# ScalarE's issue order in the attention stage: the next square and the weight casts queue behind the copies of scores, keys and x

## The chip, the cores and the metric

One core of a Trainium2 chip runs the whole kernel as one program. The metric is the device time in microseconds (us). Before the change the median of three runs is 611.57 us (609.62 to 613.83).

## The reference, cut to what matters

Three blocks follow one another, all in float32, with 4 batches, 768 tokens, 8 heads of 48 channels (d_model 384) and a hidden width of 1024:

```python
state = zeros((B, H, D, D))                         # gated linear attention
for t in range(S):
    state = alpha[:, :, t, :, None] * state + einsum('bhd,bhe->bhde', k[:, :, t], v[:, :, t])
    y[:, :, t] = einsum('bhd,bhde->bhe', q[:, :, t], state)
x = y.transpose(0, 2, 1, 3).reshape(B, S, H * D)

theta = x @ w_theta                                 # spectral block
zr, zi = x * cos(theta), x * sin(theta)
u = x + einsum('ts,bsd->btd', w_tok_r, zr) + einsum('ts,bsd->btd', w_tok_i, zi)
x = u + maximum(u @ w_ch, 0)

h = maximum(x @ w_in, 0)                            # gated block: 3-tap convolution over tokens
out = (h * sigmoid(conv3(h, conv_w))) @ w_out
```

## The kernel before, in words

**Attention by chunks.** The 24 chunks are 4 batches times 6 chunks of 128 tokens; chunk numbers below run from 0 to 23 over all batches. `a_prep` (L198) works on one chunk's keys and queries: VectorE runs two scans over the gates (L210, L215) into the tile `fbt`, of which there is one buffer, and multiplies queries and keys by them (L218). ScalarE then squares `fbt` in place and sums it (L219); the sum serves only a test of the number range at the end of the kernel, but the next chunk's first scan writes the same buffer and so comes after the square. `a_score` (L222) forms the scores on TensorE; ScalarE copies them out of PSUM into two tiles `pt` (L232; two buffers in all, so one chunk's), GpSimd masks them (L233); TensorE transposes the keys and ScalarE copies them to `kt` (L241, one buffer). `a_y` (L244) forms the chunk's output `y` from `pt`, the values and the state `S`; ScalarE copies it to `x` (L259). TensorE forms `kv`, VectorE adds it to the state (L268, tile `tst`) and GpSimd scales it into the next `S` (L273). `a_xt` (L280) transposes `x`, and ScalarE copies the transpose into `u` (L290). `a_theta` (L292) splits `u` in two float32r halves (`zh`, L71 and L72), multiplies by w_theta (`th`), and makes the two products with cosine and sine, again split (`zh`, `zl`). `m_mix` (L322) multiplies those by the token weights `wtok` into `yps`.

**Weights.** `load_split` (L105) fetches a block of 8-byte words into a `stage` tile, of which there are two, decodes it on VectorE (`decode`, L101 to L103), casts the upper half on ScalarE and forms the rest on VectorE (`split`, L70: L71 and L72). The 12 blocks of the token weights (`load_tok`, 6 for each half of the tokens) and the two of w_theta pass through the two stage tiles with the tag "st", in batch 0 and 1 of the attention. A stage tile is free for the next fetch once L72 has read it.

**Order.** In the code, `a_att(b, c)` starts the loads of chunk ci + 2, then prepares and scores chunk ci + 1, then finishes chunk ci. For batch 0 each `a_att(0, c)` is followed by `load_tok(0, c)`; for batch 1 by `load_tok(1, c)`. A planner, which simulates the program with its own cost model, turns this into one fixed queue for each engine: of the instructions that are ready it takes the one that stands first in the code. Each engine works its queue in that order, and an instruction at the head that waits holds up what stands behind it. Batches 1 to 3 of the attention are interleaved with the token mixing of the batch before; what follows 330 us holds no attention.

Of the kernel before, what the change touches and what calls it, by code (L numbers as in the profile page):

```python
# [14 lines left out]
AF = mybir.ActivationFunctionType  # L15
# [3 lines left out]
P = 128  # L19
# [24 lines left out]
def tile_gated_linear_attention__then__spectral_moe__then__conv_gate(  # L44
# [14 lines left out]
    nc = tc.nc  # L59
    NCH = B * NC  # L60

    def mm(o, lhsT, rhs, start, stop):
        nc.tensor.matmul(o, lhsT, rhs, start=start, stop=stop, skip_group_check=True)  # L63
# [4 lines left out]
        mm(o, a[1], b[0], False, stop)  # L68

    def split(hi, lo, src, lo_eng):  # L70
        nc.scalar.copy(hi, src)  # L71
        lo_eng.tensor_tensor(lo, src, hi.bitcast(F32), ALU.subtract)  # L72

    top_p = ctx.enter_context(tc.tile_pool(name="top", bufs=1))
    dram_p = ctx.enter_context(tc.tile_pool(name="xd", bufs=1, space=bass.MemoryType.DRAM))
    wmin = top_p.tile([P, NTOP], F32, name="wmin")
    bacc = top_p.tile([P, NCH], F32, name="bacc")
# [3 lines left out]
    def run(slow):  # L81
        with ExitStack() as top:
            body(top, slow)

    def body(top, slow):
# [19 lines left out]
        def load_split(pool, tag, src, shape, out_hi, out_lo, scale=None):  # L105
            n = math.prod(shape)
            st = pool.tile([P, 9 * 256], F32, tag=tag, name="stage", bufs=STB)
            d = st[:, : 2 * n].bitcast(U32)
            if len(shape) == 2:
                d = d.rearrange("p (a n) -> p a n", a=shape[0])  # L110
            nc.sync.dma_start(out=d, in_=src)
            full = st[:, 1536 : 1536 + n]
            decode(full, st, n)
            if scale is not None:
                nc.scalar.activation(full, full, AF.Copy, scale=scale)
            if len(shape) == 2:
                full = full.rearrange("p (a n) -> p a n", a=shape[0])
            split(out_hi, out_lo, full, nc.vector)

        ub, xs, zs = {}, {}, {}  # L120

# [2 lines left out]
        with ExitStack() as ph1:  # L124
# [13 lines left out]
            def load_tok(h, c):  # L138
                hs = slice(h * HALF, (h + 1) * HALF)
                load_split(  # L140
                    u_p,
                    "st",
                    w_tok[:, c * P : (c + 1) * P, hs].rearrange("i p t -> p i t").bitcast(U32),
                    [2, HALF],
                    wtok[h][0][:, :, c, :],
                    wtok[h][1][:, :, c, :],
                )
# [50 lines left out]
            def a_prep(ci):  # L198
                at, qt, vt = raw.pop(ci)
                qr = qt[:, 0:CW]  # L200
                kr = qt[:, CW : 2 * CW]
                ff = at[:, 0:CW]
                ash = at[:, 1 : CW + 1]
                ast = at[:, CW + 1 : CW + 5]
                fbt = sc_p.tile([P, 2, CW], F32, tag="fbt", name="fbt")
                fo, bf = fbt[:, 0], fbt[:, 1]
                bt = bf.rearrange("p (a t) -> p a t", a=4)
                of = onehot.rearrange("p a t -> p (a t)")
                ftot = att.tile([P, 4], F32, tag="ftot", name="ftot")
                nc.vector.tensor_tensor_scan(  # L210
                    bf[:, CW - 1 :: -1], ash[:, CW - 1 :: -1], of[:, CW - 1 :: -1], 0.0, ALU.mult, ALU.add
                )
                nc.vector.tensor_scalar(starts[:, :, 0], bt[:, :, 0], LEAST, None, ALU.max)
                nc.vector.reciprocal(starts[:, :, 0], starts[:, :, 0])
                nc.vector.tensor_tensor_scan(fo, ff, starts.rearrange("p a t -> p (a t)"), 0.0, ALU.mult, ALU.add)  # L215
                nc.vector.tensor_tensor(ftot, ast, bt[:, :, 0], ALU.mult)
                fl = fbt.rearrange("p b t -> p (b t)")
                nc.vector.tensor_tensor(qt, qt, fl, ALU.mult)  # L218
                nc.scalar.activation(fl, fl, AF.Square, accum_out=bacc[:, ci : ci + 1])  # L219
                prep[ci] = (qr.rearrange("p (a t) -> p a t", a=4), kr.rearrange("p (a t) -> p a t", a=4), ftot, vt)  # L220

            def a_score(ci):  # L222
                qh, kh, ftot, vt = prep[ci]
                scs = [ps_a.tile([P, NP, P], F32, tag="a", name="sc") for _ in range(2)]
                for p in range(NP):
                    for j in range(2):
                        r = slice(64 * j, 64 * j + D)
                        mm(scs[j][:, p, :], kh[r, p, :], qh[r, p, :], True, True)
                pts = []
                for j in range(2):  # L230
                    pt = att.tile([P, NP, P], F32, tag="pt", name="pt")
                    nc.scalar.copy(pt, scs[j])  # L232
                    nc.gpsimd.affine_select(pt, pt, [[0, NP], [1, P]], ALU.is_ge, 0.0, base=0, channel_multiplier=-1)  # L233
                    pts.append(pt)
                kt = None
                if ci % NC < NC - 1:
                    kps = ps_a.tile([P, 4, P], F32, tag="a", name="kps")
                    for p in range(NP):
                        nc.tensor.transpose(kps[:, p, :], kh[:, p, :], ident)  # L239
                    kt = att.tile([P, 4, P], F32, tag="kt", name="kt", bufs=1)  # L240
                    nc.scalar.copy(kt, kps)  # L241
                scored[ci] = (pts, kt)

            def a_y(ci):  # L244
                qh, kh, ftot, vt = prep.pop(ci)
                pts, kt = scored.pop(ci)
                c = ci % NC
                Sp, Sn = Sst[ci % 2], Sst[(ci + 1) % 2]
                y = ps_a.tile([P, DM], F32, tag="a", name="y")
                first = True  # L250
                for p in range(NP):
                    for j in range(2):
                        h = 2 * p + j
                        mm(y[:, h * D : (h + 1) * D], pts[j][:, p, :], vt[:, h * D : (h + 1) * D], first, c == 0)
                        first = False
                    if c > 0:
                        mm(y[:, p * 96 : p * 96 + 96], qh[:, p, :], Sp[:, p, :], False, True)
                x = x_p.tile([P, DM], F32, tag="x", name="x")
                nc.scalar.copy(x, y)  # L259
                xs[ci] = x  # L260
                if c < NC - 1:
                    kv = ps_a.tile([P, NP, 2 * D], F32, tag="a", name="kv")
                    for p in range(NP):
                        mm(kv[:112, p, :], kt[:, p, :112], vt[:, p * 96 : p * 96 + 96], p == 0, True)
                    nft = prep[ci + 1][2]
                    if c > 0:
                        tt = att.tile([P, NP, 2 * D], F32, tag="tst", name="tst", bufs=1)
                        nc.vector.tensor_tensor(tt[:112], Sp[:112], kv[:112], ALU.add)  # L268
                    else:
                        tt = kv  # L270
                    for j in range(2):
                        r = slice(64 * j, 64 * j + D)
                        (nc.gpsimd if c > 0 else nc.vector).tensor_tensor(  # L273
                            Sn[r, :, j * D : (j + 1) * D],
                            tt[r, :, j * D : (j + 1) * D],
                            nft[r].unsqueeze(2).to_broadcast([D, NP, D]),
                            ALU.mult,
                        )

            def a_xt(ci):  # L280
                b, c = divmod(ci, NC)
                if c == 0:
                    late = b >= B - STB
                    ub[b] = u_p.tile(
                        [P, KD, S], F32, tag="st" if late else "u", name="u", bufs=STB if late else B - STB
                    )
                xps = ps_a.tile([P, KD, P], F32, tag="a", name="xps")
                for kk in range(KD):
                    nc.tensor.transpose(xps[:, kk, :], xs[ci][:, kk * P : (kk + 1) * P], ident)
                nc.scalar.copy(ub[b][:, :, c * P : (c + 1) * P], xps)  # L290

            def a_theta(ci):  # L292
                b, c = divmod(ci, NC)
# [80 lines left out]
            for b in range(B - 1):  # L374
                for c in range(NC):
                    m_mix(b, 0, c)
                    a_att(b + 1, c)
                    if b == 0:
                        load_tok(1, c)
                for c in range(NC):  # L380
                    m_mix(b, 1, c)
                    a_theta((b + 1) * NC + c)
            att_ctx.close()
            ps_n = top.enter_context(tc.tile_pool(name="ps_n", bufs=5, space=PSUM))
            w_p = top.enter_context(tc.tile_pool(name="w2", bufs=1, side="right"))
# [271 lines left out]
```

## Time and profile before

| | |
|---|---|
| median of 3 runs | 611.57 us (609.62 to 613.83) |
| the profiled execution | 610.02 us, span of its instructions 608.3 us |
| TensorE busy, share of the span | 584.0 us, 96% |
| VectorE busy | 459.9 us, 76% |
| ScalarE busy | 333.3 us, 55% |
| GpSimd busy | 71.1 us, 12% |
| TensorE's granted clock, mean | 0.953 of full speed |

The profile is one execution. PE is TensorE's multiplications, PEld its weight loads, DVE VectorE, ACT ScalarE, POOL GpSimd, SP the queue that issues DMAs. A row of a timeline has the start in us, the length in us, the engine, the line, the operation, the tile written and the tiles read; in brackets stand the idle time of the engine before it and what ended it. PEclk is the clock granted to TensorE, where 1.00 is 2.4 GHz and 0.50 is 1.2 GHz. Matrix products of 32-bit floats are issued as two instructions each, those of float32r as one.

### The profile page before, as it was taken

The numbers are of one execution on the slowest core, as the hardware profiler recorded it, in microseconds if no ns is written. First come the engines' busy times: TensorE is split into PE (matmuls) and PEld (weight loads), VectorE is DVE, ScalarE is ACT, GpSimd is POOL, SyncE is SP. The second block draws the span as 40 slices with busy tenths as digits, with TensorE's granted clock in tenths as the row PEclk, the third lists the DMA queues.
The fourth block names the chain that finished last, engine by engine and source line by source line (L and its number), as shares of the span: only waits on it lengthen the run. The fifth ranks groups of instructions, "written<-read, shape, count | busy, mean of one in ns | idle before, by whom it ended". The sixth has DMA issues, their size and how long they took to land.

```text
span 608.3 us, 9546 instructions
## 1 busy us (share of the span) xinstructions
PE 584.0 (96%) x3703; PEld 569.2 (94%) x3703; DVE 459.9 (76%) x744; ACT 333.3 (55%) x663; POOL 71.1 (12%) x91
## 2 busy tenths in 40 slices
PE   5789999899999999999999999999999999999996
PEld 2689888799999999999999999999999999999995
DVE  7699999976764567643156888998888888888781
ACT  3436766444682446733265343666776767766571
POOL 1023621432001330112100000000000000000000
PEclk8557899899999999999999999999999999999999
DMA  8356464343102431021001333430023535445111
GB/s 297 116 176 215 151 222 127 125 138 112 62 19 77 131 119 48 15 66 61 1 0 74 110 106 105 122 138 13 27 79 117 194 118 182 148 152 194 55 41 44
DMA packets 24981, 65.33 MB, mean 107 GB/s; under 512 B 2528, under 2 KB 8672, under 8 KB 24544
## 3 DMA queue, kind: packets, MB, share of 16 engines
q1 hardware_dynamic: 24928, 64.64, 32.3%
q8 instruction: 31, 0.51, 0.3%
q14 instruction: 22, 0.18, 0.1%
HBM read 59.92 MB, written 4.72 MB: 106 GB/s over the span
## 4 chain that ended last, share of the span: by engine, by line
PE 83%; DVE 11%; DMA 2%; issue 1%; ACT 1%; POOL 1%; ACTq 0%; DVEq 0%
PE yps L63 23%; PE hps L63 17%; PE ops L63 16%; PE y L63 8%; PE cps L63 6%; PE th L63 5%; PE sc L63 3%; PE kv L63 2%; DMA stage<-in_w_tok_dram 2%; DVE fbt L215 2%; DVE fbt L210 1%; PE kps L239 1%; DVE qk_t L218 1%; DVE stage L102 1%; DVE wtok L72 1%
## 5 line engine op out<-in xcount | busy, mean ns | idle before, releaser
L63 PE MATMUL yps<-wtok,zh 128*128 128x384 f32 x576 | 151.6, 343 | 1.0 <-ACT zh L71 1.0
L63 PEld LDWEIGHTS yps<-wtok,zh 128*128 128x128 f32 x576 | 105.9, 192 | 1.7 <-ACT zh L71 1.4
L63 PE MATMUL hps<-x,win 128*128 128x386 f32 x576 | 107.1, 339 | 0.0
L63 PE MATMUL ops<-wout,g 128*128 128x384 f32 x576 | 106.9, 338 | 0.0
L63 PEld LDWEIGHTS hps<-x,win 128*128 128x128 f32 x576 | 102.2, 189 | 0.0
L63 PEld LDWEIGHTS ops<-wout,g 128*128 128x128 f32 x576 | 101.7, 187 | 0.0
L63 PE MATMUL yps<-wtok,zl 128*128 128x384 f32 x288 | 97.9, 344 | 0.0
L233 POOL TENSOR_SCALAR_AFFINE_SELECT pt<-pt 128x512 f32<-128x512 f32 x48 | 46.0, 981 | 214.9 <-ACT pt L232 214.9
L63 PE MATMUL y<-v_t,pt 128*128 128x48 f32 x384 | 59.2, 286 | 0.0
L63 PEld LDWEIGHTS y<-v_t,pt 128*128 128x128 f32 x384 | 56.3, 213 | 0.5
L63 PEld LDWEIGHTS yps<-wtok,zl 128*128 128x128 f32 x288 | 55.2, 192 | 0.0
L219 ACT ACTIVATE fbt<-fbt 128x1024 f32<-128x1024 f32 x24 | 25.4, 1059 | 52.8 <-DVE qk_t L218 52.5
L479 ACT ACTIVATE cv<-cv 128x384 f32<-128x384 f32 x64 | 33.4, 523 | 31.0 <-DVE cv L476 30.9
L72 DVE TENSOR_TENSOR g<-cv,g 128x384 fp32r<-128x384 f32 x64 | 35.4, 555 | 15.1 <-ACT g L71 14.5
L63 PE MATMUL th<-wth,zh 128*128 128x384 f32 x216 | 44.3, 348 | 0.0
L232 ACT COPY pt<-sc 128x512 f32<-128x512 f32 x48 | 25.7, 585 | 29.7 <-PE y L63 29.7
L210 DVE TENSOR_TENSOR_SCAN fbt<-a_t,onehot 128x512 f32<-128x512 f32 x24 | 29.7, 1236 | 16.3 <-ACT fbt L219 14.4
L63 PEld LDWEIGHTS sc<-qk_t 48*128 48x128 f32 x384 | 28.6, 204 | 14.0 <-issue 7.5
L63 PE MATMUL sc<-qk_t 48*128 48x128 f32 x384 | 33.8, 304 | 8.0 <-DVE qk_t L218 8.0
L473 DVE SCALAR_TENSOR_TENSOR cv<-hh,cw,cv 128x383 f32<-128x383 f32 (+1 forms) x64 | 38.3, 612 | 4.1 <-ACT cv L470 3.8
L63 PE MATMUL y<-S,qk_t 128*128 128x96 f32 x160 | 37.5, 319 | 3.9 <-POOL S L273 3.9
L480 DVE SCALAR_TENSOR_TENSOR cv<-cv,hh 128x384 f32<-128x384 f32 x64 | 35.2, 555 | 7.9 <-ACT cv L479 5.9
(84 smaller groups left out, 903.5 us busy)
## 6 DMA issues: line engine op xcount, KB each, us to landing
qk_t<-in_qka_dram SPq DMA_DIRECT2D x24, 512.0 KB, 3.7
stage<-in_w_tok_dram SPq DMA_DIRECT2D x12, 768.0 KB, 4.9
top<-in_w_tok_dram SPq DMA_DIRECT2D x12, 768.0 KB, 4.3
a_t<-in_qka_dram SPq DMA_DIRECT2D x24, 260.0 KB, 2.8
v_t<-in_v_dram SPq DMA_DIRECT2D x24, 192.0 KB, 3.3
out_dram<-ob SPq DMA_DIRECT2D x24, 192.0 KB, 1.9
stage<-in_w_in_dram SPq DMA_DIRECT2D x4, 768.0 KB, 5.1
stage<-in_w_out_dram SPq DMA_DIRECT2D x4, 768.0 KB, 4.3
```

The costliest lines, as they stand in the source:

```text
L63: nc.tensor.matmul(o, lhsT, rhs, start=start, stop=stop, skip_group_check=True)
L72: lo_eng.tensor_tensor(lo, src, hi.bitcast(F32), ALU.subtract)
L102: nc.vector.scalar_tensor_tensor(fb, hi, 0xC0000000, fb, ALU.bitwise_and, ALU.bitwise_or)
L210: nc.vector.tensor_tensor_scan(bf[:, CW - 1 :: -1], ash[:, CW - 1 :: -1], of[:, CW - 1 :: -1], 0.0, ALU.mult, ALU.add)
L215: nc.vector.tensor_tensor_scan(fo, ff, starts.rearrange("p a t -> p (a t)"), 0.0, ALU.mult, ALU.add)
L218: nc.vector.tensor_tensor(qt, qt, fl, ALU.mult)
L219: nc.scalar.activation(fl, fl, AF.Square, accum_out=bacc[:, ci : ci + 1])
L232: nc.scalar.copy(pt, scs[j])
L233: nc.gpsimd.affine_select(pt, pt, [[0, NP], [1, P]], ALU.is_ge, 0.0, base=0, channel_multiplier=-1)
L473: nc.vector.scalar_tensor_tensor(cv[:, a:HALF], hh[:, o + a - 1 : o + HALF - 1], cw[:, f, 0:1], cv[:, a:HALF], ALU.mult, ALU.add)
L479: nc.scalar.activation(cv, cv, AF.Tanh, scale=0.5)
L480: nc.vector.scalar_tensor_tensor(cv, cv, 1.0, hh[:, o : o + HALF], ALU.add, ALU.mult)
```

## The change: four copies are marked, and two kinds of instruction queue behind the marks

While the program is traced, the last copy to `pt` (L232, the second of the chunk's two), the last copy to `kt` (L241), to `x` (L259) and to `u` (L290) are remembered. Each square (L219) and each cast of a weight block with the tag "st" (L71 of `load_split`) gets an edge to those four as they stand when it is traced. The edge is of a kind that the planner honours as an order in the queue; it adds no semaphore, since all these instructions run on ScalarE. No instruction is added or removed. By the order of the code, the square of chunk n comes behind pt and kt of chunk n-1 and x and u of chunk n-2; the cast of `load_tok(0, c)` behind pt and kt of chunk c+1 and x and u of chunk c; the cast of `load_tok(1, c)` behind pt and kt of chunk c+7 and x and u of chunk c+6; the casts of w_theta behind pt and kt of chunk 1 and x and u of chunk 0.

```diff
     def split(hi, lo, src, lo_eng):
-        nc.scalar.copy(hi, src)
+        cast = nc.scalar.copy(hi, src)
         lo_eng.tensor_tensor(lo, src, hi.bitcast(F32), ALU.subtract)
+        return cast
+
+    marks = {}
+
+    def behind(ins, keys):
+        for k in keys:
+            if k in marks:
+                tc.add_manual_dep(
+                    ins.ins,
+                    marks[k].ins.name,
+                    mybir.DependencyInfo(mybir.DependencyClass.NoSync, mybir.DependencyReason.DATA),
+                    reason="issue order",
+                )
...
-            split(out_hi, out_lo, full, nc.vector)
+            cast = split(out_hi, out_lo, full, nc.vector)
+            if tag == "st" and not slow:
+                behind(cast, ("pt", "kt", "x", "u"))
...
-                nc.scalar.activation(fl, fl, AF.Square, accum_out=bacc[:, ci : ci + 1])
+                sq = nc.scalar.activation(fl, fl, AF.Square, accum_out=bacc[:, ci : ci + 1])
+                behind(sq, ("pt", "kt", "x", "u"))
...
-                    nc.scalar.copy(pt, scs[j])
+                    marks["pt"] = nc.scalar.copy(pt, scs[j])
...
-                    nc.scalar.copy(kt, kps)
+                    marks["kt"] = nc.scalar.copy(kt, kps)
...
-                nc.scalar.copy(x, y)
+                marks["x"] = nc.scalar.copy(x, y)
...
-                nc.scalar.copy(ub[b][:, :, c * P : (c + 1) * P], xps)
+                u_copy = nc.scalar.copy(ub[b][:, :, c * P : (c + 1) * P], xps)
+                if not slow:
+                    marks["u"] = u_copy
...
+            marks.clear()
             att_ctx.close()
```

## Rows read from the trace of the kernel before

**Rows 1.** Windows: busy us (instructions) of PE, PEld, DVE, ACT, POOL; PEclk, DMA, GB/s

```profile
25.00:120.00 95.00, 86.40 (x567) 81.96 (x568) 92.41 (x129) 52.60 (x98) 31.56 (x24) 0.81 0.56 176
120.00:370.00 250.00, 250.00 (x1742) 244.53 (x1741) 155.80 (x239) 121.34 (x234) 35.19 (x53) 0.99 0.22 70
```

**Rows 2.** Timeline of ACT, 34 to 42 us: start, length, what

```profile
34.39 1.06 ACT L219 ACTIVATE fbt<-fbt 128x1024 f32<-128x1024 f32 x1 [7.13 <-DVE qk_t L218]
...
36.17 1.06 ACT L232 COPY pt<-sc 128x512 f32<-128x512 f32 x2
37.12 0.49 ACT L259 COPY x<-y 128x384 f32<-128x384 f32 x1
```

**Rows 3.** Waits of PE, whole span: total us, times, longest us

```profile
PE y L63 <- POOL S L273: 3.9, 2, 2.5
PE xps L289 <- ACT x L259: 2.8, 2, 1.8
...
PE yps L63 <- ACT zh L71: 1.0, 1, 1.0
PE kv L63 <- ACT pt L232: 0.7, 1, 0.7
```

**Rows 4.** Timeline of PE, 34 to 38 us

```profile
34.20 1.70 PE L63 MATMUL kv<-v_t,kt 128*112 128x96 f32 x8
37.66 0.90 PE L289 MATMUL xps<-ident,x 128*128 128x128 f32 x3 [1.76 <-ACT x L259]
```

**Rows 5.** Windows (columns as in Rows 1) that follow the two waits for S

```profile
70.00:77.00 7.00, 7.00 (x29) 7.00 (x28) 6.97 (x11) 4.87 (x9) 3.96 (x4) 0.51 0.90 278
118.00:125.00 7.00, 7.00 (x31) 7.00 (x31) 6.93 (x9) 3.82 (x7) 4.32 (x4) 0.52 0.43 142
```

**Rows 6.** The chain of waits that ended last, 106 to 113 us: start, length, what

```profile
106.40 0.79 PE kv L63 x8
...
112.13 0.56 DVE tst L268
...
112.77 2.69 POOL S L273
```

**Rows 7.** Line L273, the update of S: ns min/median/max, first and last start

```profile
L273 POOL TENSOR_TENSOR S<-tst,ftot x32: 498/505/2682, 43.2 to 294.7; 48x192 f32<-48x192 f32 x32
```

**Rows 8.** Groups, 8 to 120 us: count, busy us, mean ns, idle before

```profile
L102 DVE SCALAR_TENSOR_TENSOR stage<-stage 128x768 uint32<-128x768 uint32 x13 | 12.5, 960 | 0.0
L210 DVE TENSOR_TENSOR_SCAN fbt<-a_t,onehot 128x512 f32<-128x512 f32 x10 | 12.5, 1247 | 1.5 <-ACT fbt L219 1.5
...
L72 DVE TENSOR_TENSOR wtok<-stage,wtok 128x768 fp32r<-128x768 f32 x11 | 11.5, 1048 | 0.0
...
L218 DVE TENSOR_TENSOR qk_t<-qk_t,fbt 128x1024 f32<-128x1024 f32 x9 | 11.4, 1263 | 0.1
```

**Rows 9.** Timeline of ACT: two weight casts and the copies to u

```profile
20.99 0.83 ACT L71 CAST wth<-stage 128x768 fp32r<-128x768 f32 x1
...
23.68 0.48 ACT L290 COPY u<-xps 128x384 f32<-128x384 f32 x1
...
67.58 0.82 ACT L71 CAST wtok<-stage 128x768 fp32r<-128x768 f32 x1
...
88.95 0.46 ACT L290 COPY u<-xps 128x384 f32<-128x384 f32 x1
```

**Rows 10.** Waits of DVE, 0 to 100 us

```profile
DVE stage L101 <- DMA stage<-in_w_tok_dram: 2.0, 2, 1.7
```

**Rows 11.** Timeline of POOL and, below it, of PE in batch 1

```profile
142.09 1.08 POOL L273 TENSOR_TENSOR S<-tst,ftot 48x192 f32<-48x192 f32 x2
...
147.26 0.43 PE L63 MATMUL y<-S,qk_t 128*128 128x96 f32 x2
```

**Rows 12.** Timeline of PE in batch 2: one chunk's xps and the next chunk's scores

```profile
202.06 0.49 PE L289 MATMUL xps<-ident,x 128*128 128x128 f32 x3
...
211.62 1.16 PE L63 MATMUL sc<-qk_t 48*128 48x128 f32 x16
```

## The prediction, made before the changed kernel was run

> **What bounds the kernel now.** I read the busy shares and the slices first, then the windows by stage, then the chain of waits, and last the queues of ScalarE and TensorE instruction by instruction. The windows show two regimes [rows 1]. Between 25 and 120 us VectorE is busy 92.41 of 95 us, so its queue paces the stage; TensorE is busy 86.40 us, at a mean clock of 0.81 of full speed. From 120 to 370 us TensorE is busy for all 250 us at 0.99 while VectorE has 94 us free: there ScalarE's order cannot make anything earlier, it can only break something. So whatever the change gives must come ahead of 120 us, where TensorE lost 8.6 us idle and, of the 86.40 us busy, about 16 us to the low clock (86.40 x 0.19).
>
> In the queue of ScalarE the reader is to see what the edit takes aim at [rows 2]. At 34.39 us the square of chunk 3 runs, after 7.13 us in which ScalarE stood still for VectorE's product; behind it in the queue stand the copies of chunk 2's scores and of chunk 1's x. TensorE's waits list what that cost it over the whole kernel: 2.8 us for x, 1.0 us for a cast to zh, 0.7 us for scores [rows 3]. They are small, and they are all that ScalarE makes TensorE wait. The other wait is for the state S, 3.9 us, and it drags the clock along: in the 7 us that follow each of its two occurrences the granted clock is at 1.2 GHz nearly throughout [rows 5].
>
> **The change, part by part.**
>
> *The squares.* 24 of them, 1.06 us each [rows 8], none added. Chunk 3's goes from ahead of pt and x to behind u of chunk 1. In the row of TensorE the kv products end at 35.90 us (34.20 + 1.70) and the transpose of x starts only at 37.66 us, after 1.76 us of waiting [rows 4]. With the square out of the way, pt can start when y ends, near 34 us, and x is there some 1.6 us later (1.06 + 0.49), before kv ends. **Gain 1.8 us.** The other waits of this kind are 1.0 us for zh and 0.7 us for pt [rows 3]; in the timeline a square stands ahead of both in ScalarE's queue, and ahead of pt a weight cast too: **gain 1.7 us.** The remaining 1.0 us of the wait for x lies in chunk 0, where TensorE waits for the product of chunk 2 right afterwards; I count nothing.
>
> *What is queued behind the square.* The next chunk's first scan needs the buffer that the square reads. In the steady state the transposes of one chunk end at 202.55 us, and the scores of the chunk three further on start at 211.62 us [rows 12]. In between must now fit: u 0.46 us [rows 9], the square 1.06 us [rows 2] and its sum 0.2 us, two scans of about 1.25 us and the product 1.26 us [rows 8], and the small operations between the scans, 0.5 us as I estimate from the same timeline: 6.0 us. The margin is 3.1 us of 9.1 per chunk. So the square costs nothing while other work of VectorE inside that chain stays under 3.1 us; the cover is TensorE's mixing products, and if it is gone each chunk pays the excess. In this kernel the chain has had a free run: preparations were up to two chunks ahead, and now they are one ahead.
> The loads of queries and keys are issued by SP in the same fixed order as the fetches of weight blocks; a fetch that waits for a stage tile holds the loads behind it, so the shorter lead is shared by that queue. GpSimd's queue is not moved past, only its inputs come sooner.
>
> *The casts of w_theta.* The first, at 20.99 us, must go behind u of chunk 0, which ends at 24.16 us [rows 9]. The subtraction behind it frees a stage tile, so the first fetch of token weights, and VectorE's decode, come about 1.1 us later; VectorE already waits 2.0 us for these fetches [rows 10]. On the other side pt, x and kt of chunks 0 and 1 come 0.8 us sooner, and the product of chunk 2 need not queue behind that subtraction. Between -0.9 and +1.2 us; I take **a loss of 1.1 us**, since the row that is nearest is that of the wait for the fetch.
>
> *The casts of token weights.* 12, 0.82 us each. The first needs copies that are long done and stays; the others go later, the sixth most: from 67.58 us to behind u of chunk 5, 88.95 us [rows 9]. Each cast holds its stage tile, and so SP's next fetch of a block, and so a decode and a subtraction of VectorE: two operations of 0.96 us, one of 1.05 us [rows 8] and a shift of some 0.6 us, 3.6 us per block. By the positions of u in the queue, about 2.5 blocks fewer are through by 116 us: 9 us of VectorE's work leave the stretch where VectorE is the bound and come in the next, where it has a third of its time free. The products do not miss the blocks: in the timeline the mixing of the first half of the tokens reaches its sixth block only after 108 us and that of the second half its first near 150 us, and the last block's cast waits for u of chunk 11, at 154.6 us, some 10 us ahead of its own products.
>
> What this frees cannot all arrive, because TensorE, busy 86.40 of the 95 us, is the near second there [rows 1]. What it can do is bring the state update sooner. Near 113 us GpSimd's scaling of S took 2.69 us [rows 6] where half of the 32 took 0.51 us or less [rows 7], beside decodes and a scan on VectorE, and the addition ahead of it ran at 112.13 us although kv was done at 107.19 us [rows 6]: 4.9 us in VectorE's queue behind decode and scan. TensorE stood still 2.5 us [rows 3] and then ran 7 us at 0.52 [rows 5], which costs 7 x 0.48 = 3.4 us. I expect that one to go: **gain 5.9 us** (between 0 and 5.9). Its twin near 67 us (1.3 us of waiting and 7 x 0.49 = 3.4 us of clock) I leave in: there the stage tiles are still full. New waits of VectorE and TensorE, from the shorter lead of the preparations, I bound by 0 and 6 us (two stalls like the 2.5 us one, with some clock) and take **2 us lost**, nearer to the small ones of the list.
>
> *Sum:* -1.8 - 1.7 + 1.1 - 5.9 + 2.0 = -6.3 us. The profiled execution took 610.02 us (span 608.3 us and 1.7 us around it), so 603.7 us; the median of the three runs stands 1.5 us above that execution, which makes **605 us**.
>
> **The rivals.**
>
> *A, the forecast, 0.42.* As summed, 600 to 609 us.
>
> *B, nothing to speak of, 0.24.* VectorE paces the stage, its work is the same, and the edges only change which of its inputs is late. Then only the 3.5 us of direct waits come, less the 1.1 us of the fetch, and the S stall stays: 609 us; 606 to 614. For it: VectorE idles 2.6 of 95 us [rows 1]. Against it: which work it does before 116 us does change.
>
> *C, slower, 0.22: the moved decodes hold the later updates of S.* From 120 to 155 us a pair of updates of S takes 1.08 us, and y reads S 4.1 us after the end (147.26 - 143.17) [rows 11]. The second half's blocks, decoded between 77 and 120 us before, now come between 100 and 150 us, next to just those updates, and the shorter lead makes scans meet them too. An update with the 2.69 us of [rows 6], 2.2 us over the usual, in a queue of VectorE that is 2 us late, passes the 4.1 us of slack, and then TensorE stops 2.5 us and loses 3.4 us of clock. Two such stalls give 610.0 - 3.5 + 1.1 + 2 x 5.9 = 619.4 us with the old one kept as well, and 621 us by the median; the point is a decode pair right beside the update. Against it: the planner sees this work and TensorE's clock stays high through the stretch now. The Trainium skill has a rule that speaks for this rival, "SBUF — State Buffer", section "Who interferes with whom": a VectorE instruction with two SBUF inputs contends with a GpSimd instruction that reads SBUF, and the loser blocks rather than sharing. By that rule the 2.69 us update agrees, and every decode moved beside an update repeats it.
>
> *D, both S stalls go, 0.12.* If the attention of batch 0 also runs freer, the 4.7 us near 67 us go as well: 597 to 601 us.
>
> That the change does little of what it says is part of B: the planner may already have put most squares behind the copies, as it has in batch 2, where the square follows a product that is late anyway.
>
> **How the numbers follow.** About 1% (6 us) is what a measurement of this kernel can tell from no change. Faster by more than that, below 605.5 us: all of D and six tenths of A, 0.12 + 0.25, rounded to 0.38. Within 1%: the rest of A and nearly all of B, 0.40. Slower: C, 0.22. The likeliest case alone gives 600 to 609 us; the range reaches from D's better half, 598 us, to the lower part of C, 619 us, and leaves out a tenth on either side.
>
> **What would show it.** Right: squares in the trace of the changed kernel start after u of two chunks before; TensorE's waits for x, zh and pt fall from 4.5 us to near 1; no wait for S near 113 us, and no dip of the clock at 118 us; the last cast of token weights moves from 119 us to 140 us or later; VectorE shows its first idle time before 110 us. Wrong in A's step: a stall for S at another chunk with the clock falling behind it, or TensorE waiting for the product of L218 after 30 us, which would say that the margin of 3.1 us was not there. Wrong altogether: an idle TensorE after 120 us.

## The result: 603.74 us, 1.3% faster, and the profile after

The changed kernel takes **603.74 us** (median of 4 runs, 602.09 to 604.70) beside 610.91 us (609.62 to 613.83, 4 runs) of the kernel before on the same chip: a ratio of **0.987, 95% interval 0.983 to 0.992**. Forecast were 605 us, in a range of 598 to 619. The profiled execution took 604.70 us, the highest of the four, with a span of 602.8 us. One execution among all the runs (676.94 us, at a mean granted clock of 0.782, in the first run of "Where in the attention the edges work") is of a slower state of the chip, and no ratio counts it.

Until the first product of the last block (`hps`) the profiled execution before took 370.13 us and this one 364.61 us; what comes behind took 238.2 us in both. The theta work that ends batch 1's attention starts its long run of products at 149.29 us instead of 154.59 us, so 5.3 of these 5.5 us were won before 155 us. Ahead of 112 us nothing was won: the scores of chunk 9 start at 112.02 us before and at 112.13 us after, with 603 and 607 products done. The next transpose, that of chunk 8, starts at 127.01 us before and at 120.85 us after. TensorE between the two points, first before, then after:

```profile
112.02 1.16 PE L63 MATMUL sc<-qk_t 48*128 48x128 f32 x16
116.69 0.46 PE L63 MATMUL y<-S,qk_t 128*128 128x96 f32 x2 [2.54 <-POOL S L273]
127.01 0.49 PE L289 MATMUL xps<-ident,x 128*128 128x128 f32 x3
```

```profile
112.13 1.16 PE L63 MATMUL sc<-qk_t 48*128 48x128 f32 x16
114.10 0.43 PE L63 MATMUL y<-S,qk_t 128*128 128x96 f32 x2
120.85 0.49 PE L305 MATMUL xps<-ident,x 128*128 128x128 f32 x3
```

That stretch took 14.99 us and takes 8.72 us: 6.3 us less, all of the gain and a little more.

Windows of the kernel after (length, busy us and instructions of PE, PEld, DVE, ACT, POOL; then PEclk, DMA, GB/s), the two of [rows 1] and the two of [rows 5]:

```profile
25.00:120.00 95.00, 90.75 (x596) 86.14 (x597) 84.19 (x120) 51.64 (x98) 28.41 (x26) 0.81 0.50 158
120.00:370.00 250.00, 249.51 (x1744) 243.79 (x1744) 167.30 (x255) 125.43 (x238) 39.52 (x51) 1.00 0.25 83
70.00:77.00 7.00, 7.00 (x34) 7.00 (x34) 5.83 (x7) 3.45 (x7) 3.01 (x3) 0.54 0.63 209
118.00:125.00 7.00, 6.87 (x58) 6.42 (x57) 6.86 (x11) 2.87 (x6) 2.52 (x4) 1.00 0.71 248
```

Between 25 and 120 us VectorE is busy 8.2 us less than in [rows 1] and TensorE 4.4 us more, with 29 products more done; behind 120 us VectorE is busy 11.5 us more. The dip of the clock behind 118 us is gone (0.52 before, 1.00 now); the one behind 70 us has stayed (0.51 and 0.54).

Waits of TensorE in the kernel after (total us, times, longest us), against [rows 3]:

```profile
PE sc L63 <- DVE qk_t L233: 7.6, 3, 4.0
PE xps L305 <- ACT x L275: 3.0, 2, 2.7
PE wps L381 <- DVE onehot L188: 1.8, 1, 1.8
PE y L63 <- POOL S L289: 1.5, 2, 1.1
```

The waits for zh (1.0 us) and pt (0.7 us) have left the list, that for S fell from 3.9 to 1.5 us, and that for x has not fallen: its longest grew from 1.8 to 2.7 us. ScalarE's and TensorE's queues where [rows 2, 4] were read (timelines after: start, length, what, idle time before and its releaser) show why:

```profile
35.40 0.83 ACT L71 CAST wtok<-stage 128x768 fp32r<-128x768 f32 x1 [9.10 <-DVE stage L116]
36.14 1.06 ACT L248 COPY pt<-sc 128x512 f32<-128x512 f32 x2
37.09 0.49 ACT L275 COPY x<-y 128x384 f32<-128x384 f32 x1
...
38.58 0.48 ACT L306 COPY u<-xps 128x384 f32<-128x384 f32 x1 [0.51 <-PE xps L305]
38.96 0.83 ACT L71 CAST wtok<-stage 128x768 fp32r<-128x768 f32 x1
39.69 1.06 ACT L234 ACTIVATE fbt<-fbt 128x1024 f32<-128x1024 f32 x1
```

```profile
33.25 1.70 PE L63 MATMUL kv<-v_t,kt 128*112 128x96 f32 x8
37.64 0.91 PE L305 MATMUL xps<-ident,x 128*128 128x128 f32 x3 [2.69 <-ACT x L275]
```

The square of chunk 3 has moved from 34.39 us to 39.69 us, behind u, as the edge says. But a cast of the first block of token weights stands ahead of pt, and ScalarE stood still 9.10 us for its decode. x and the transpose come at the times of before.

Near 113 us VectorE and GpSimd of the kernel after, against [rows 6]; TensorE then read S at 114.10 us without a wait:

```profile
104.64 0.96 DVE L72 TENSOR_TENSOR zl<-zf,zh 128x768 fp32r<-128x768 f32 x1 [0.63 <-ACT zh L71]
105.75 0.96 DVE L72 TENSOR_TENSOR wtok<-stage,wtok 128x768 fp32r<-128x768 f32 x1 [0.15 <-ACT wtok L71]
106.80 1.22 DVE L225 TENSOR_TENSOR_SCAN fbt<-a_t,onehot 128x512 f32<-128x512 f32 x1
...
108.48 1.40 DVE L230 TENSOR_TENSOR_SCAN fbt<-a_t,starts 128x512 f32<-128x512 f32 x1
109.92 1.47 DVE L233 TENSOR_TENSOR qk_t<-qk_t,fbt 128x1024 f32<-128x1024 f32 x1
111.42 0.56 DVE L284 TENSOR_TENSOR tst<-S,kv 112x384 f32<-112x384 f32 x1
111.89 0.55 DVE L359 TENSOR_TENSOR u<-yps,u 128x384 f32<-128x384 f32 x1
112.36 0.62 DVE L114 TENSOR_SCALAR stage<-stage 128x768 uint32<-128x768 uint32 x1
112.90 0.55 DVE L359 TENSOR_TENSOR u<-yps,u 128x384 f32<-128x384 f32 x1
```

```profile
112.06 1.29 POOL L289 TENSOR_TENSOR S<-tst,ftot 48x192 f32<-48x192 f32 x2 [1.75 <-DVE tst L284]
```

The same place in the kernel before:

```profile
112.77 3.87 POOL L273 TENSOR_TENSOR S<-tst,ftot 48x192 f32<-48x192 f32 x2 [3.48 <-DVE tst L268]
113.07 0.95 DVE L103 SCALAR_TENSOR_TENSOR stage<-stage 128x768 uint32<-128x768 uint32 x1
113.94 1.22 DVE L210 TENSOR_TENSOR_SCAN fbt<-a_t,onehot 128x512 f32<-128x512 f32 x1
```

VectorE had idle moments before 106 us, and no decode stands between scan, product and addition any more. The addition runs 0.7 us earlier than in [rows 6], but the larger part is the pair of scalings, which takes 1.29 us where it took 3.87 us. With a pair of 1.29 us the kernel before would have had S at 114.06 us (112.77 + 1.29), and TensorE stood ready for it at 114.15 us (116.69 - 2.54): the longer pair accounts for the wait. What had changed beside it is VectorE's work, a decode and a scan before, two additions of `yps` (in PSUM) and a shift after; that these neighbours set the pair's length is read from the rows and was not tried by itself.

### The profile page after: what moved, and what is told of

The parts are those of the page before. It is cut to its first block, busy times and chain, and to the rows that moved or that the text cites. A ratio compares the mean times of both kernels' runs of the same rounds, so it can differ in the third digit from the quotient of the medians.

```text
span 602.8 us, 9563 instructions
## 1 busy us (share of the span) xinstructions
PE 582.6 (97%) x3703; PEld 567.2 (94%) x3703; DVE 459.6 (76%) x744; ACT 334.2 (55%) x663; POOL 72.2 (12%) x91
## 4 chain that ended last, share of the span: by engine, by line
PE 82%; DVE 11%; DMA 2%; ACT 2%; POOL 1%; issue 1%; DVEq 0%; ACTq 0%
PE yps L63 22%; PE hps L63 17%; PE ops L63 17%; PE y L63 8%; PE cps L63 6%; PE th L63 5%; PE sc L63 3%; PE kv L63 2%; DVE fbt L230 2%; DVE qk_t L233 2%; DVE fbt L225 2%; PE kps L255 1%; POOL S L289 1%; DMA stage<-in_w_tok_dram 1%; PE xps L305 1%
## 5 line engine op out<-in xcount | busy, mean ns | idle before, releaser
L63 PE MATMUL yps<-wtok,zh 128*128 128x384 f32 x576 | 149.1, 340 | 0.1
L63 PEld LDWEIGHTS yps<-wtok,zh 128*128 128x128 f32 x576 | 104.0, 189 | 0.4 <-ACT zh L71 0.2
L63 PE MATMUL cps<-us,wch 128*128 128x384 f32 x216 | 40.0, 338 | 0.0
L489 ACT ACTIVATE cv<-hh,cw 128x384 f32<-128x384 f32 x64 | 38.3, 615 | 2.2 <-DVE g L72 1.9
```

Source lines behind the costliest of these rows:

```text
L489: nc.scalar.activation(cv, hh[:, o : o + HALF], AF.Copy, scale=cw[:, f, 1:2])
```

## The experiments

The ratios below are medians against runs of the kernel before on the same chip, whose medians were 610.9 to 611.8 us in all four groups of runs. The theories, as the expectations number them:

1. The forecast's: later casts mean later decodes, VectorE's queue is free near 113 us, and the stall for S with its loss of clock goes. The squares add only their direct waits.
2. ScalarE's copies, no longer behind squares, make the gain.
3. Any new plan of the queues gives another luck; nothing in it belongs to the edges.
4. Formed after the first group: the two parts are needed together. Late casts take decodes out of VectorE's queue, late squares take preparations out of it; with one alone, the other kind of work moves up into the freed place.
5. Named in two later expectations: the first half of the token-weight casts carries the gain, or one plan's luck does.

In all of them I split TensorE's time up to the first `hps` product in windows of 2 us: idle time, busy time lost to the clock (busy x (1 - PEclk)) and the rest. The rest was 327 to 331 us in every profile, so idle time and clock tell a kernel's time to within some 4 us. Each row is one execution, which the last columns set beside the median of its kernel; two executions of the same queues can differ by as much as the kernels do (last section), so verdicts go by the medians:

| | idle | lost to the clock | first `hps` at | this execution | median |
|---|---|---|---|---|---|
| before | 18.3 | 23.7 | 370.13 | 610.02 | 610.91 |
| after | 14.2 | 20.6 | 364.61 | 604.70 | 603.74 |
| squares only | 25.2 | 16.1 | 369.68 | 609.91 | 614.05 |
| casts only | 19.1 | 25.0 | 373.60 | 614.04 | 614.27 |
| after, S on VectorE | 20.8 | 11.0 | 361.97 | 602.56 | 603.15 |
| before, S on VectorE | 21.0 | 27.5 | 377.12 | 617.89 | 614.67 |
| after, first cast later | 15.1 | 15.6 | 361.72 | 601.42 | 599.92 |
| after, stall put back | 15.2 | 20.0 | 365.68 | 605.97 | 607.38 |

### Each part alone

The squares alone:

```diff
-            if tag == "st" and not slow:
-                behind(cast, ("pt", "kt", "x", "u"))
```

> Only the squares queue behind the copies; the weight casts keep their old freedom. Theory 1 (the casts keep the stage tiles, so decodes leave VectorE's queue before 113 us, and the wait for S near 113 us goes): the decodes stay early, a wait for S of 2 to 3 us near 113 us stays with 7 us at 1.2 GHz behind it, 608 to 612 us, ratio 0.995 to 1.002. Theory 2 (the copies freed from the squares carry the gain): 602 to 605 us, ratio 0.985 to 0.99. Theory 3 (any new plan shifts the wait away by chance): no telling, anything from 602 to 612 us.

Measured: **614.05 us** (609.91 to 617.40, 12 runs), ratio 1.002 [0.999, 1.006]: nothing, and by the median slower than any theory had put it. The decodes keep their early places, and now the preparations are late too (the square of chunk 9 at 118.2 us, 111.3 us before). Waits of TensorE, 25 to 160 us, in the profiled execution, the fastest of the twelve:

```profile
PE xps L303 <- ACT x L273: 4.7, 2, 4.3
PE y L63 <- POOL S L287: 4.2, 3, 2.1
PE sc L63 <- DVE qk_t L231: 4.1, 2, 2.6
PE yps L63 <- ACT zh L71: 2.3, 2, 1.5
PE yps L63 <- DVE zl L72: 2.2, 1, 2.2
```

Its wait for S near 113 us has shrunk to 0.34 us, but scores waited 1.50 us just ahead of it, at 118.26 us, and other waits came at earlier places. Theory 2 falls with this run.

The casts alone:

```diff
-                behind(sq, ("pt", "kt", "x", "u"))
```

> Only the weight casts queue behind the copies; the squares keep their old freedom. Theory 1: no wait for S over 1 us between 100 and 130 us and the clock stays at 2.4 GHz there, 602 to 606 us, ratio 0.985 to 0.992. Theory 2: the waits for scores and x stay, 608 to 611 us, ratio 0.995 to 1.0. Theory 3: anything from 602 to 612 us.

Measured: **614.27 us** (610.73 to 615.54, 12 runs), ratio 1.003 [1.001, 1.006]: nothing won, and outside all three ranges. Theory 1 is half right: in the trace the addition of chunk 7 runs at 110.43 us, TensorE has no stall for S near 113 us, and between 60 and 120 us it loses 6.7 us to idle time and clock where the kernel before lost 10.1 us. But these 3.4 us are given back later. TensorE in this kernel, timeline:

```profile
135.75 0.46 PE L63 MATMUL y<-S,qk_t 128*128 128x96 f32 x2 [0.92 <-POOL S L288]
...
168.68 0.98 PE L63 MATMUL yps<-wtok,zh 128*128 128x384 f32 x2 [2.76 <-DVE u L358]
```

and windows that follow the two waits:

```profile
136.00:144.00 8.00, 8.00 (x49) 8.00 (x49) 7.47 (x12) 4.11 (x8) 3.22 (x3) 0.79 0.29 62
168.00:172.00 4.00, 3.32 (x11) 3.35 (x12) 3.73 (x9) 3.12 (x8) 0.00 (x0) 0.57 0.02 4
```

The clock falls behind each (8.00 x 0.21 = 1.7 us and 3.32 x 0.43 = 1.4 us). The last two squares, free, run at 150.15 and 156.10 us, 6.0 us apart (in the kernel after 141.23 and 150.58 us, 9.4 apart), so the preparations run beside the work on theta, and the mixing's addition to u stands in VectorE's queue behind both and what they held up. The kernel before has its last squares as close (146.42 and 152.10 us), but no weight block left to cast there. This link is read from the timeline and was not tried by itself. After 120 us this kernel loses 8.0 us, the one before 2.3.

### Which engine scales S

If GpSimd's slow scaling beside VectorE's operations is the cause of the stall, VectorE doing it should free both kernels.

```diff
-                        (nc.gpsimd if c > 0 else nc.vector).tensor_tensor(
+                        nc.vector.tensor_tensor(
```

In the kernel after:

> The changed kernel with the scaling of S on VectorE for every chunk in place of GpSimd (two operations of some 0.35 us each). The one wait for S that is left, 1.1 us at 69.6 us, and the 7 us at 1.2 GHz behind it (3.4 us) should go, against about 0.7 us more of VectorE's work for each of some 8 chunks before 120 us. If the wait with its clock is worth what theory 1 counts (4.5 us): 597 to 602 us, ratio 0.978 to 0.986. If VectorE's longer queue takes it back: 602 to 606 us, ratio 0.986 to 0.992.

Measured: **603.15 us** (602.56 to 604.49, 6 runs), ratio 0.985 [0.981, 0.989], the time of the kernel after. The clock is full from 40 us on, no wait for S is left, and 9.6 us less are lost to the clock; but 6.6 us more are idle, with waits for x of 6.8 us in 5 between 25 and 160 us. Ahead of x in ScalarE's queue four of these five have activations of theta (L330 to L332), the first of which waited 2.86 to 4.01 us for VectorE; the fifth has the first token-weight cast. VectorE took back what it gave. How much of the clock's share is the edit's stays open (last section).

In the kernel before:

> The kernel before with the scaling of S on VectorE for every chunk, and nothing of the change. Both waits for S (1.3 and 2.5 us) and both stretches at 1.2 GHz (3.4 us each) should go: up to 10.7 us, less some 4 us of VectorE's longer queue. If the wait at 113 us with its clock is what the change removed: 600 to 606 us, ratio 0.982 to 0.992, so as fast as the changed kernel or faster, without a cast moved. If the change's gain has another root: 608 to 612 us.

Measured: **614.67 us** (609.78 to 618.77, 12 runs), ratio 1.003 [1.000, 1.007]. A miss: 600 to 606 us were expected. The stall near 113 us is gone here too, yet the profile, of an execution of 617.89 us, has 2.7 us more idle and 3.8 us more lost to the clock, with new waits of mixing products for zh (3.9 us in 2). A stall taken away by loading VectorE buys nothing while VectorE's queue is the one that is full.

For chunk 7 alone, in the kernel before:

```diff
-                        (nc.gpsimd if c > 0 else nc.vector).tensor_tensor(
+                        (nc.gpsimd if c > 0 and ci != 7 else nc.vector).tensor_tensor(
```

> The kernel before with only one update of S, that behind chunk 7, on VectorE in place of GpSimd; up to there the plan is that of before. If the wait at 113 us with its clock is worth 5.9 us: no wait there, the clock stays at 2.4 GHz from 112 to 126 us, 604 to 607 us, ratio 0.988 to 0.994. If another wait takes its place a little later: 609 to 612 us.

Measured: **610.92 us** (608.72 to 615.73, 12 runs), ratio 1.000 [0.997, 1.003]. TensorE and the window around it in this kernel:

```profile
115.89 0.58 PE L63 MATMUL y<-S,qk_t 128*128 128x96 f32 x2 [1.24 <-DVE S L273]
```

```profile
112.00:126.00 14.00, 12.76 (x77) 12.39 (x77) 13.82 (x22) 5.50 (x11) 4.80 (x4) 0.76 0.31 107
```

The wait fell from 2.5 to 1.24 us and the clock dipped as before. The scaling now stood in VectorE's own queue, at 115.14 us, behind the same decode and scan beside which GpSimd's pair had taken 3.87 us. On either engine it is what VectorE has queued at that moment that makes S late.

### The stall put back

```diff
+                    if ci == 7:
+                        scr = att.tile([P, NP, 2 * D], F32, tag="scr", name="scr", bufs=1)
+                        for j in (0, 1, 0, 1, 0, 1):
+                            r = slice(64 * j, 64 * j + D)
+                            nc.gpsimd.tensor_tensor(
+                                scr[r, :, j * D : (j + 1) * D],
+                                tt[r, :, j * D : (j + 1) * D],
+                                nft[r].unsqueeze(2).to_broadcast([D, NP, D]),
+                                ALU.mult,
+                            )
```

> The changed kernel with six more products on GpSimd (into a scratch tile) ahead of the update of S behind chunk 7, about 3 us or more, so that the wait for S near 113 us is there again. If that wait and the clock behind it are what the change removed: TensorE waits 2 to 4 us for S near 114 us, 7 us at 1.2 GHz follow, and the time is 607 to 611 us, ratio 0.994 to 1.0. If the gain has another root: 603 to 605 us.

Measured: **607.38 us** (605.97 to 607.87, 6 runs), ratio 0.992 [0.990, 0.995]. That is 3.6 us over the kernel after by the medians, 3.0 us by the two ratios, whose intervals still overlap. TensorE and the window around it:

```profile
114.43 0.46 PE L63 MATMUL y<-S,qk_t 128*128 128x96 f32 x2 [1.80 <-POOL S L299]
```

```profile
112.00:126.00 14.00, 12.20 (x91) 11.75 (x89) 12.67 (x17) 5.68 (x11) 9.72 (x10) 0.88 0.42 130
```

1.80 us of waiting and 12.20 x 0.12 = 1.5 us of clock: 3.3 us, worked out as the forecast priced such a stall, from wait and clock. VectorE's and ScalarE's queues are those of the kernel after, instruction by instruction. From the scores of chunk 9 to the transpose of chunk 8 this kernel takes 12.29 us (110.50 to 122.79), the kernel after 8.72 us: 3.6 us more. At the first `hps` product only 1.1 us of that is seen (365.68 and 364.61 us), because this execution was 1.6 us ahead at the scores of chunk 9, on the same queues, with 2.3 us less lost to the clock before 60 us.

### Where in the attention the edges work

The second half's casts and all squares:

```diff
-        def load_split(pool, tag, src, shape, out_hi, out_lo, scale=None):
+        def load_split(pool, tag, src, shape, out_hi, out_lo, scale=None, late=False):
...
-            if tag == "st" and not slow:
+            if late and not slow:
                 behind(cast, ("pt", "kt", "x", "u"))
...
+                    late=h == 1,
```

> Of the changed kernel, the edges of the squares and of the six casts of the second half of the token weights; the casts of w_theta and of the first half are free again. Theory 4 (both parts are needed together near 113 us and after: the late second half empties VectorE's queue there, the late squares keep the preparations from filling it again): no wait for S over 1 us from 100 to 160 us, 602 to 606 us, ratio 0.985 to 0.992. Theory 5 (it is the first half, or any one plan's luck): 608 to 615 us.

Measured: **605.23 us** (median of 7, six of which took 604.04 to 606.11), ratio 0.988 [0.986, 0.991]. Its profile is that of the execution left out above, and no row of it is used.

The same, with the squares of chunks 8 to 14 alone:

```diff
-                behind(sq, ("pt", "kt", "x", "u"))
+                if 8 <= ci <= 14:
+                    behind(sq, ("pt", "kt", "x", "u"))
```

> Only the six casts of the second half and the squares of chunks 8 to 14, so the edges between some 90 and 160 us alone. Theory 4 (late second half plus late preparations empty VectorE's queue around the updates of S): the additions before S come at even distances of some 9 us from 111 us on, no wait for S over 1 us from 100 to 160 us, 603 to 607 us, ratio 0.986 to 0.994. If the squares of batch 0 are needed as well: 609 to 614 us, ratio 0.997 to 1.004.

Measured: **602.79 us** (600.61 to 604.92, 6 runs), ratio 0.985 [0.981, 0.988], the whole gain. The addition of chunk 7 runs at 111.19 us right behind scan and product, y read S at 115.45 us without a wait, and the clock is 1.00 from 112 us on. The queues of VectorE, ScalarE and GpSimd are those of the kernel before up to 82 us; near 71 us its wait for S is longer (3.0 us, 1.3 before), so the gain lies behind.

A control: only the squares of chunks 16 to 23; the edges of the casts are taken out as above.

```diff
-                behind(sq, ("pt", "kt", "x", "u"))
+                if ci >= 16:
+                    behind(sq, ("pt", "kt", "x", "u"))
```

> A control for luck of the plan: only the squares of chunks 16 to 23 get the edges, where TensorE is busy throughout. Theories 1 and 4: nothing, 609 to 613 us, ratio 0.997 to 1.003, with both waits for S and both stretches at 1.2 GHz as before. Theory 3 (any disturbance of the plan moves the time by a per cent): something else.

Measured: **613.29 us** (608.69 to 615.70, 12 runs), ratio 1.001 [0.999, 1.004]. The stall is there, 2.54 us at 120.78 us. The queues of its four engines are those of the kernel before up to 190 us, so the run tells that edges behind that point give nothing, and little about other plans ahead of it. Against theory 3 stands the whole set: four plans that differ from the one before from some point ahead of 117 us and lack one or both kinds of edges (squares only, casts only, and the two with S on VectorE) have ratios of 1.000 to 1.003, and every kernel with both kinds is faster. It doesn't exclude that part of the difference between plans is luck, since each edit makes a new plan.

The first half's casts and those of w_theta, with all squares:

```diff
-        def load_split(pool, tag, src, shape, out_hi, out_lo, scale=None):
+        def load_split(pool, tag, src, shape, out_hi, out_lo, scale=None, early=True):
...
-            if tag == "st" and not slow:
+            if tag == "st" and early and not slow:
                 behind(cast, ("pt", "kt", "x", "u"))
...
+                    early=h == 0,
```

> The other half of the casts: w_theta and the first half of the token weights, and all squares; the second half's casts are free. Theory 4: the second half is decoded early again, the wait for S near 113 us or one like it is back, 608 to 614 us, ratio 0.995 to 1.004. Theory 5 (the first half carries the gain): 603 to 606 us.

Measured: **606.00 us** (602.30 to 608.40, 6 runs), ratio 0.990 [0.987, 0.993]. A miss for theory 4 as I had put it, which placed the gain in the second half's casts alone; it lies at the edge of theory 5's range. But the first half is not needed either, by the two runs before the control: either half of the casts with the squares brings most of the gain. How the first half does it is open. The profiled execution was the slowest of the six; there the addition of chunk 7 came at 110.10 us and S kept TensorE waiting only 0.4 us, but scores waited 1.8 us for the product of L218 ahead of it and the clock was 0.63 from 112 to 126 us.

### The cast that stayed in the way

The prediction's step on x failed by the first cast of token weights. Tracing its load one chunk later gives its edge newer marks:

```diff
-                load_tok(0, c)
+                else:
+                    if c == 1:
+                        load_tok(0, 0)
+                    load_tok(0, c)
```

> The changed kernel with the first block of token weights traced one chunk later, so that its cast stands behind the scores of chunk 2 too. The cast that now stands at the head of ScalarE's queue for 9.1 us, waiting for a decode, should no longer hold those scores and x of chunk 1: TensorE's wait of 2.7 us at 37.6 us should go. If it is worth its length: 600 to 602 us, ratio 0.981 to 0.985. If VectorE is late with the next product anyway: 602 to 605 us, as the changed kernel.

Measured: **599.92 us** (598.49 to 601.42, 5 runs), ratio 0.980 [0.977, 0.982], better than both kernels. ScalarE and TensorE of this kernel where the 9.10 us stood:

```profile
32.45 1.07 ACT L248 COPY pt<-sc 128x512 f32<-128x512 f32 x2 [6.32 <-PE y L63]
33.40 0.50 ACT L275 COPY x<-y 128x384 f32<-128x384 f32 x1
...
35.83 0.85 ACT L71 CAST wtok<-stage 128x768 fp32r<-128x768 f32 x1
```

```profile
33.08 1.70 PE L63 MATMUL kv<-v_t,kt 128*112 128x96 f32 x8
34.57 0.85 PE L305 MATMUL xps<-ident,x 128*128 128x128 f32 x3
35.07 2.89 PE L63 MATMUL th<-wth,zh 128*128 128x384 f32 x9
```

The transpose starts at 34.57 us, 3.1 us earlier, and TensorE does not stop between 26 and 40 us. Its clock rises at 37 us and not near 53 us; new waits for S (3.2 us in 3) come later, and the clock falls again near 44 and 54 us, behind two of them (1.64 us at 42.21 us, 1.34 us at 53.70 us). Of 3.8 us gained by the medians 2.9 us stand in the first `hps` product's start. The wait is gone by the edit; whether the early rise is the edit's, one execution can't tell.

With S on VectorE as well:

```diff
-                        (nc.gpsimd if c > 0 else nc.vector).tensor_tensor(
+                        nc.vector.tensor_tensor(
```

> The first block of token weights traced one chunk later, as in the run where its cast moved, and S scaled on VectorE for every chunk. If the waits for S that are left (3.2 us) and the clock behind them go at the price of VectorE's longer queue: 594 to 599 us, ratio 0.972 to 0.979. If VectorE takes it back, as in the kernel before: 599 to 604 us.

Measured: **606.33 us** (602.64 to 609.71, 7 runs), ratio 0.991 [0.987, 0.994]: outside both ranges, and worse than the later cast alone (0.980); against S on VectorE alone (0.985 [0.981, 0.989]) the intervals overlap. In its profiled execution (608.83 us) 4.1 us of this stand behind the first `hps` product, where no edit works (242.3 us, 238.2 in the kernel after). Waits for zh came (3.13 us at 75.00 us), as in the kernel before with S on VectorE. The two edits do not add.

## Why the prediction was right, and where its steps were not

**The S stall near 113 us, -5.9 us: it came as priced.** No wait at 114.10 us, the clock stays full, and the stretch from the scores of chunk 9 to the transpose of chunk 8 is 6.3 us shorter. In the profiles TensorE's idle time between 60 and 160 us fell by 3.8 us and the loss to the clock by 3.4 us. The stall put back cost 3.0 to 3.6 us for a wait of 1.80 us.

**The sum, -6.3 us: near, in part by luck.** The four other terms were to add up to -0.4 us. Each was off, and in the profiles they come to +0.1 us up to the scores of chunk 9 and +0.6 us behind the stall, so the stall is the whole of it. The medians fell by 7.2 us, the two profiled executions by 5.3 us.

**Its reason was half of the reason.** I put the step down to the casts: 9 us of VectorE's work leave the stretch. They do: VectorE is busy 84.19 of the 95 us and not 92.41 us, and the last token-weight cast ran at 149.84 us, not 119.11 us. But the casts alone gained nothing, and I had counted the squares as direct waits of ScalarE only. What the squares hold back is the next scan, and so the preparation. That both are needed is shown by the runs; by which operations of VectorE is read from the timelines. Nor does S come sooner mainly because the addition does (0.7 us): the pair of scalings, beside other work of VectorE, shrank from 3.87 to 1.29 us. In the kernel after, the additions to the state from chunk 7 on come at 111.42, 120.92, 130.04 and 139.33 us, each 9.1 to 9.5 us behind the last; before, 112.13, 122.91, 132.65 and 141.41 us.

**The wait for x, -1.8 us: wrong.** The timeline had two instructions ahead of pt that waited for VectorE, the square and a cast, and I named the one that moved. The edge of the cast points at copies long done, as the prediction itself says further on ("The first needs copies that are long done and stays"), so its wait of 9.10 us took the square's place, and TensorE's wait grew from 1.76 to 2.69 us. With that cast out of the way x came 3.1 us earlier.

**The waits for zh and pt, -1.7 us: gone, but not seen in the time.** Both have left the list, and TensorE is idle 2.1 us less up to the scores of chunk 9; these still start at 112.13 us and not at 112.02 us. TensorE's busy time up to there is 2.2 us more, 0.2 us of it by the clock and a part by four more products; the rest is open.

**The fetch of token weights, +1.1 us: right as a delay, wrong as a loss.** It was issued at 26.02 us, before at 24.96 us, but the decode started only 0.3 us later (30.92 and 30.61 us), and the products of theta for chunk 2 start at 52.34 us, before at 52.36 us. The scores of chunk 2 came 0.95 us sooner (25.27 and 26.22 us), the gain that I had put at up to 0.9 and not counted.

**New waits, +2 us: smaller.** They are the 0.9 us more for x and, after 120 us, 0.5 us of idle time; the margin of 3.1 us in the chain of square, scans and product held.

**The twin near 67 us stayed**, as said: 1.09 us of waiting, 7 us at 0.54. There GpSimd's row shows the other end of the scale, a pair of scalings beside back-to-back operations of VectorE:

```profile
63.98 5.61 POOL L289 TENSOR_TENSOR S<-tst,ftot 48x192 f32<-48x192 f32 x2 [0.96 <-DVE tst L284]
```

**The rivals.** C, the slower one, was right in its mechanism and wrong in its price: behind 120 us pairs of scalings take 1.93 to 2.10 us, where two of the three before took 1.08 us [rows 11], but y waits for S only once there, 0.36 us at 132.82 us, since VectorE's additions come early enough. The Trainium skill says of this in "SBUF — State Buffer", section "Who interferes with whom", that a GpSimd instruction which reads SBUF can be blocked by one of VectorE with two SBUF inputs. The rows agree: the same pair took 1.08 us twice while VectorE stood still but for 0.4 us, 3.87 us beside the decode and the scan above, and 5.61 us beside a row of six such operations. B fell with the stall at 113 us; D did not come, as the twin stayed.

## What to carry to other kernels

An edge that only reorders an engine's queue is to be judged by the engine behind it: here most of its worth was which decodes and scans VectorE has queued when the state is updated; ScalarE's own order counted where an instruction stood at the head of its queue and waited (9.10 us). Look at everything that stands ahead of a late instruction, not at the one the edit moves; what remains takes over the wait. And of two edits that each empty a queue, neither may show anything alone, since the other kind of work moves up.

## What the runs showed of the hardware that was not expected

TensorE's clock stayed at 1.2 GHz through 14 us (38 to 52 us) in which TensorE was busy without a gap, in the kernel before; the last 12 of them:

```profile
40.00:44.00 4.00, 4.00 (x20) 3.56 (x19) 3.59 (x6) 2.69 (x5) 0.73 (x2) 0.50 1.00 319
44.00:48.00 4.00, 4.00 (x21) 3.78 (x19) 4.00 (x7) 1.00 (x2) 0.47 (x1) 0.50 0.92 319
48.00:52.00 4.00, 4.00 (x22) 4.00 (x21) 4.00 (x6) 3.66 (x9) 1.03 (x1) 0.50 0.10 13
```

It rose there near 53 us. In the kernel with the squares alone it rose near 44 us, though TensorE had stood still from 36 to 40 us, and in the kernel after with S on VectorE near 40 us, though it had stood still for 1.2 of the 2 us from 34 us. The rise is not set by the plan. In three profiles the queues of TensorE, VectorE, ScalarE and GpSimd are the same, instruction by instruction, up to 112 us (the kernel before, the one with S of chunk 7 on VectorE, the control), and the clock rose near 53, 41 and 41.5 us. Nor is an early rise a gain in itself while VectorE paces the stage: up to 112 us the second of the three lost 7.3 us less to the clock than the first and was idle 5.1 us more, and its scores of chunk 9 start at 112.09 us, those of the first at 112.02 us and those of the third at 116.11 us. So a good part of the spread of the kernel before, of which 29 runs in one group took 608.48 to 615.29 us, can come from executions of one plan. What decides when the clock rises these runs do not tell.
